# A planned attention kernel: prologue shared by two engines and two queues, projections mixed in and bunched, last norm and last residual divided

## The chip, the cores and the metric

The kernel runs on one core of one Trainium2 chip. The metric is the device time of one execution in microseconds (us); medians are of three to nine executions. Besides the time, each execution has a span (first to last instruction of the core) and a mean granted clock of TensorE. Differences below one microsecond in the times are not read as anything here.

Engine names in the profile: PE is TensorE, PEld its weight loads, DVE VectorE, ACT ScalarE, POOL GpSimd, SP SyncE.

## The reference

```python
x  = A_x                                   # [1, 2048, 512] bf16
xn = layernorm(x)                          # over the 512 columns, eps 1e-5
q  = (xn @ wq) as 32 heads of 16           # wq 512 x 512
k, v = xn @ wk, xn @ wv                    # one k and one v for all heads, 512 x 16
p  = softmax(q k^T / 4)                    # 32 heads, 2048 x 2048
s  = (p v, heads side by side) @ wo        # wo 512 x 512
h  = silu(xn @ w1)                         # w1 512 x 1792
g  = silu(h @ w2)                          # w2 1792 x 512
return x + s * g
```

## The kernel before

The kernel does not write its instructions in program order. It holds tasks with estimated durations, a clock for each engine, and rules that choose what comes next; from the resulting order it writes the instructions of each engine and the semaphores between them. So a constant in a rule moves thousands of instructions. What is planned is this work:

- Scores: 32 heads by 4 blocks of 512 queries by 16 tiles of 128 keys, in all 2048 "slots" of 128 keys by 512 queries. One score phase of TensorE makes three or four slots at once, each in a quarter of the array's rows.
- Exponentials: a real Exp on ScalarE into one of `NPA` buffers, or a fast path (VectorE writes the bits of a bf16 exponential, GpSimd adds three shifted copies, so that one slot then needs four PV matmuls instead of one).
- PV: "rounds" of four matmuls that fill four column strips of one bank.
- Projections q, h (first of the feed-forward), z (second) and w (output): "jobs" made of rounds of the same four-column kind.

```python
MM = 216.0                                  # ns of a round or a score phase
NEAR, AHEAD = 12, 0.6
NPA, PRESS = 22, 16                         # buffers of P; number in use at which PV goes first
NDB, NDS = 6, 8                             # buffers of fast-path bits, of shifted copies
START_Z, START_H = 8, 14                    # a job starts only below this number of P buffers in use
WIDE, NMIN, EARLY = 2, 3, 200.0             # banks that one Exp may take
...
def s_mm(pe, b, g, i, kt):                  # one slot's scores
    return pe.matmul(bank(b), lhsT=kt_sb[32 * i:32 * i + 32, g % 2, kt * P:(kt + 1) * P],
                     rhs=qt_sb[32 * i:32 * i + 32, (g // 2) % NQR, :],
                     start=True, stop=True, tile_position=(32 * i, 0))

def col4(h, b, lhs, rhs, start, stop, n=NQ):    # one round
    for j in range(4):
        last = h.matmul(bank(b)[32 * j:32 * (j + 1), 0:n], lhsT=lhs(j), rhs=rhs, start=start, stop=stop,
                        tile_position=(0, 32 * j), skip_group_check=True)
    return last
```

The prologue loads x, normalises 16 token tiles in four groups (statistics, reciprocal root, xn; then TensorE transposes it and projects k, v and the first q). Keys come free group by group, and with them slots:

```python
for t in range(4):
    dma(SP, "x", x_tile(t), xv[:, t, :], 128, [xkey(t)], prio=0)
...
for t in range(4):
    mk_T([t], t)          # transposes of xn, token tile t
mk_K(0, 0, 1, 4)          # k of tile 0
mk_q(0)                   # q of the first 512 queries, after all four tiles
mk_K(0, 1, 4, 3)          # k of tiles 1 to 3
mk_V(0)
for c in range(1, NC):    # the other three groups of keys
    mk_T([4 * c, 4 * c + 1]); mk_T([4 * c + 2, 4 * c + 3])
    mk_K(c, 4 * c, 4 * c + 4)
    mk_V(c)
NPRO = len(jobs)          # jobs start in the order of the list: projections only after all of these
```

TensorE's rule, at every step: a score phase if one can go and ScalarE will need it; otherwise one round, chosen so:

```python
if pr and pr[0] == "go" and (a_pressure() >= PRESS or closing()):
    col = ("pv", pr[1])
elif jr[0] == "go":
    col = ("job", jr[1])
elif pr and pr[0] == "go":
    col = ("pv", pr[1])
elif tr and tr[0] == "go":
    col = ("tail", None)
elif t_done and not tail["made"]:
    ...                   # filler: matmuls on zeros, meant to keep TensorE busy
```

The tail: after the last PV the last 512 queries are normalised (transpose, reciprocal, product, transpose on VectorE), the output projection of four token tiles follows, then VectorE scales and adds the residual, and four stores end it:

```python
tail["items"].sort(key=lambda x: (x[0], x[1], x[2]))   # 12 rounds with o < 3 first, then four with o = 3
...
t1 = Task(DV, T_P, lambda v: v.scalar_tensor_tensor(out=fin_sb[:, k, :], in0=bank(b), scalar=0.25,
          in1=tmp_sb[:, tt % 8, :], op0=ALU.mult, op1=ALU.mult), ...)
t2 = Task(DV, 333.0, lambda v: v.tensor_tensor(ob_sb[:, tt % 4, :], fin_sb[:, k, :], xr_sb[:, tt % 4, :], ALU.add), ...)
```

The softmax here doesn't subtract the row's maximum and nothing guards it: scores larger than these inputs give would overflow.

## Time and profile before

| | before |
|---|---|
| median of 3 | 684.39 us (684.32 to 685.62) |
| span of the profiled execution | 684.2 us, clock 0.996 |
| busy TensorE, ScalarE, VectorE, GpSimd | 98, 96, 88, 80% |
| first Exp | 13.31 us |
| first score phase after 48 slots, "slot 48" below (all keys nearly in use) | 38.57 us |
| slot 2020 issued (28 left, this one included) | 661.52 us |
| last PV begins, span ends | 674.83, 684.2 us |

The prediction below shows the page's totals, stretches and waits of this kernel. Two views more are used later. First the chain that ended last, by engine: the work, followed back from the end, lies on TensorE for 54% of the span and on ScalarE for 35%, so by this view neither is the sole owner.

```profile
PE 54%; ACT 35%; DVE 9%; issue 1%; DMA 1%; SPq 0%; DVEq 0%
```

The time line: start, length, engine, line, operation, output from inputs, shapes, count, and in brackets the idle time before with what ended it.

### The profile page before, as it was taken

What the parts mean: (1) busy time and instruction counts of PE and PEld (TensorE: products, weight loads), DVE (VectorE), ACT (ScalarE), POOL (GpSimd) and SP (SyncE); (2) the same over time, 40 slices, a digit from 0 to 9 for tenths busy, and PEclk for the clock granted to TensorE, in tenths of its full rate; (3) what the DMA queues carried; (4) which work ended last, traced back from release to release, by engine and by line L of the source; (5) the groups of instructions that cost most, each with busy time, mean ns of one, the idle gap of its engine ahead of it and who ended that gap; (6) DMA issues with size and microseconds to landing.
All of it is one profiled execution on the core that took longest, in us unless ns stands there. A gap on an engine that the chain in (4) does not pass through costs nothing.

```text
span 684.2 us, 21033 instructions
## 1 busy us (share of the span) xinstructions
PE 668.1 (98%) x8887; PEld 191.7 (28%) x8887; DVE 603.0 (88%) x1064; ACT 658.8 (96%) x763; POOL 548.8 (80%) x545
## 2 busy tenths in 40 slices
PE   8899999999999999999999999999999999999995
PEld 3422222222222222222222222222222222222221
DVE  9889999898899998988989899899889999898863
ACT  4899999999999999999999999999999999999994
POOL 2059989789998878889878788889999778899980
PEclk9999999999999999999999999999999999999999
DMA  9300000000000010000000100000000010000000
GB/s 307 128 17 2 3 2 2 2 2 2 2 2 17 18 33 1 2 2 2 2 2 1 34 17 17 2 2 1 2 2 2 2 33 16 17 3 2 2 2 32
DMA packets 11436, 12.65 MB, mean 18 GB/s; under 512 B 1808, under 2 KB 10768, under 8 KB 11344
## 3 DMA queue, kind: packets, MB, share of 16 engines
q1 hardware_dynamic: 10288, 11.28, 5.1%
q8 instruction: 72, 1.18, 0.7%
q10 hardware_dynamic: 1056, 0.03, 0.1%
q14 instruction: 20, 0.16, 0.1%
HBM read 8.95 MB, written 2.10 MB: 16 GB/s over the span
## 4 chain that ended last, share of the span: by engine, by line
PE 54%; ACT 35%; DVE 9%; issue 1%; DMA 1%; SPq 0%; DVEq 0%
ACT pa_sb L1365 33%; PE ps L1103 22%; PE ps L789 19%; PE ps L479 14%; DVE db_sb L975 4%; ACT t_sb L601 2%; DVE stats_sb L426 1%; DVE f_sb L1120 1%; DVE u_sb L603 1%; DMA ds_sb<-in_A_x_dram 1%; DVE xn_sb L455 0%; DVE otr_sb L1124 0%; DVE xnT_sb L506 0%; DVE tmp_sb L603 0%; SPq L373 0%
## 5 line engine op out<-in xcount | busy, mean ns | idle before, releaser
L1042 POOL INT64_ADD ds_sb<-db_sb x534 | 544.9, 1040 | 117.8 <-DVE db_sb L975 65.2
L1365 ACT ACTIVATE pa_sb<-ps 128x1024 bf16<-128x1024 f32 (+1 forms) x684 | 630.5, 1027 | 6.8 <-PE ps L789 6.3
L975 DVE TENSOR_SCALAR db_sb<-ps 128x512 uint16<-128x512 f32 x712 | 468.6, 684 | 61.4 <-PE ps L789 57.7
L1103 PE MATMUL ps<-ds_sb,v_sb 128*32 128x512 bf16 x2136 | 277.5, 383 | 0.0
L789 PE MATMUL ps<-qt_sb,kt_sb 32*128 32x512 bf16 x2048 | 258.0, 385 | 4.9 <-ACT pa_sb L1365 1.7
L1103 PE MATMUL ps<-pa_sb,v_sb 128*32 128x512 bf16 x1336 | 244.6, 384 | 1.4 <-ACT pa_sb L1365 1.4
L1103 PE MATMUL ps<-db_sb,v_sb 128*32 128x512 bf16 x712 | 186.5, 384 | 1.1 <-DVE f_sb L1120 1.1
L789 PEld LDWEIGHTS ps<-qt_sb,kt_sb 32*128 32x128 bf16 x2048 | 64.2, 91 | 283.3 <-ACT pa_sb L1365 181.8
L1103 PEld LDWEIGHTS ps<-ds_sb,v_sb 128*32 128x32 bf16 x2136 | 69.1, 95 | 54.0 <-issue 35.3
L479 PE MATMUL ps<-xnT_sb,w_sb 128*32 128x512 bf16 x896 | 75.4, 385 | 0.0
L479 PE MATMUL ps<-w_sb,u_sb 128*32 128x512 bf16 x896 | 73.1, 384 | 0.0
L1103 PEld LDWEIGHTS ps<-pa_sb,v_sb 128*32 128x32 bf16 x1336 | 60.5, 95 | 44.5 <-issue 29.9
L1103 PEld LDWEIGHTS ps<-db_sb,v_sb 128*32 128x32 bf16 x712 | 46.3, 95 | 22.3 <-issue 14.5
L601 ACT ACTIVATE t_sb<-ps 128x512 bf16<-128x512 f32 x72 | 45.3, 629 | 0.0
L603 DVE SCALAR_TENSOR_TENSOR u_sb<-t_sb,ps 128x512 bf16<-128x512 bf16 x56 | 38.1, 681 | 1.5 <-ACT t_sb L601 0.2
L1120 DVE STREAM_TRANSPOSE f_sb<-ps 128x512 f32<-128x512 f32 x32 | 22.6, 707 | 9.3 <-PE ps L1103 9.2
L479 PEld LDWEIGHTS ps<-xnT_sb,w_sb 128*32 128x32 bf16 x896 | 17.9, 94 | 26.9 <-issue 22.0
L479 PEld LDWEIGHTS ps<-w_sb,u_sb 128*32 128x32 bf16 x896 | 16.9, 94 | 26.3 <-issue 24.5
L479 PE MATMUL ps<-xnT_sb,wq_sb 128*32 128x512 bf16 x256 | 21.0, 392 | 0.0
L479 PE MATMUL ps<-wo_sb,on_sb 128*32 128x512 bf16 x256 | 20.8, 383 | 0.1
L1124 DVE TENSOR_TENSOR otr_sb<-f_sb,rcp_sb 128x256 bf16<-128x256 f32 x32 | 13.3, 417 | 0.3
L603 DVE SCALAR_TENSOR_TENSOR tmp_sb<-t_sb,ps 128x512 bf16<-128x512 bf16 x16 | 10.8, 677 | 2.0 <-ACT t_sb L601 1.9
(52 smaller groups left out, 140.4 us busy)
## 6 DMA issues: line engine op xcount, KB each, us to landing
w_sb<-in_B_w_dram SPq DMA_DIRECT2D x2, 1792.0 KB, 12.8
xr_sb<-in_A_x_dram SPq DMA_DIRECT2D x16, 128.0 KB, 2.3
out_dram<-ob_sb SPq DMA_DIRECT2D x16, 128.0 KB, 1.7
ds_sb<-in_A_x_dram SPq DMA_DIRECT2D x3, 512.0 KB, 7.1
ds_sb<-in_A_x_dram SPq DMA_DIRECT2D x4, 128.0 KB, 2.5
wq_sb<-in_A_wq_dram SPq DMA_DIRECT2D x1, 512.0 KB, 4.9
wo_sb<-in_A_wo_dram SPq DMA_DIRECT2D x1, 512.0 KB, 14.6
kt_sb<-kt_sb SPq DMA_DIRECT2D x4, 64.0 KB, 2.3
```

Source lines behind the costliest of these rows:

```text
L426: ts_ = pl.add(Task(DV, 593.0, lambda v, t=t: v.bn_stats(stats_sb[:, t, :], x_tile(t)), [xkey(t)], [("st", t)], 1 + j, gate=(lambda: q_don ...
L479: last = h.matmul(bank(b)[32 * j:32 * (j + 1), 0:n], lhsT=lhs(j), rhs=rhs, start=start, stop=stop, tile_position=(0, 32 * j), skip_group_c ...
L601: t1 = Task(AC, 490.0, lambda a: a.activation(t_sb[:, k, :], src, ACT.Tanh, scale=scale), [held], [("t", k)], 0, [t0])
L603: t2 = Task(DV, T_P, lambda v: v.scalar_tensor_tensor(out=dst, in0=t_sb[:, k, :], scalar=1.0, in1=src, op0=ALU.add, op1=ALU.mult), [held, ...
L789: return pe.matmul(bank(b), lhsT=kt_sb[32 * i:32 * i + 32, g % 2, kt * P:(kt + 1) * P], rhs=qt_sb[32 * i:32 * i + 32, (g // 2) % NQR, :], ...
L975: bt.P[i] = pl.add(Task(DV, T_P, lambda v, b=b, i=i, bb=bt.b: v.tensor_scalar(db_sb[:, bb, i * NQ:(i + 1) * NQ], bank(b), 128.0 * LOG2E, 1 ...
L1042: whole["po"].append(pl.add(Task(PO, T_P64, lambda g, cols=cols: g.int64_add(ds_sb[:, s, cols].bitcast(U64), db_sb[:, bt.b, cols].bitcast( ...
L1103: h = pe.matmul(bank(OB)[32 * i:32 * (i + 1), :], lhsT=lhs, rhs=rhs, start=s0, stop=s1, tile_position=(0, 32 * i), skip_group_check=True)
L1120: t1 = pl.add(Task(DV, T_TR, lambda v: v.transpose(f_sb[:, k, :], bank(OB)), [("ps", OB)], [("F", k)], 1, [norm.get(("m", g - 2))]))
L1124: t3 = pl.add(Task(DV, 332.0, lambda v: v.tensor_tensor(o3[:, :, val:val + DH], f3[:, :, val:val + DH], rcp_sb[:, k, :].unsqueeze(2).to_br ...
L1365: op = pl.place(AC, 0.8333 * NQ * n + T_AF, lambda a: a.activation(pa_sb[:, s * NQ:(s + n) * NQ].rearrange("p (b n) -> p b n", n=NQ), ps3[ ...
```

## The change

Its intent: start the first Exp and each later group of keys sooner by taking work off VectorE in the prologue and putting feed-forward rounds into TensorE's idle time there; plan the middle with more P buffers and with projections in bunches (fewer changes of layout); shorten the tail by splitting the last norm and by letting TensorE and ScalarE add the residual of three tiles. A random factor with a fixed seed on some thresholds picks one plan of many. Left out of the cut below are another bank for the PV sums (7 for 6) and new time estimates of the planner (450 ns for issuing a DMA, where it had 60). The diff, cut to its core:

```diff
+J_BASE, J_END, MIXJ = 0.1, 1.0, 2
+SEED, SPREAD = 17, 0.1
-NEAR, AHEAD = 12, 0.6
+NEAR, AHEAD = 18, 0.6
-NPA, PRESS = 22, 16
-NDB, NDS = 6, 8
+NPA, PRESS = 26, 16
+PRESS_Z, PRESS_H = 18, 16
+NDB, NDS = 5, 8
-START_Z, START_H = 8, 14
-WIDE, NMIN, EARLY = 2, 3, 200.0
+START_Z, START_H = 6, 8
+WIDE, NMIN, EARLY = 3, 3, 200.0
 ...
-            dma(SP, "x", x_tile(t), xv[:, t, :], 128, [xkey(t)], prio=0)
+            dma((SP, AC)[t % 2], "x", x_tile(t), xv[:, t, :], 128, [xkey(t)], prio=-2)
 ...  # statistics of tile 1 on ScalarE: sum by Copy, sum of squares by Square
+        m1 = pl.add(Task(AC, 700.0, lambda a: a.activation(f_sb[:, 0, :], x_tile(1), ACT.Copy, scale=1.0 / D,
+                                                          accum_out=mv_sb[:, 1, 0:1]), ...
 ...  # q of the first queries per token tile, copied by ScalarE; two xnT copies on ScalarE, not three
-        for t in range(4):
-            mk_T([t], t)
+        mk_T([0], 0)
+        mk_T([1], 1)
         mk_K(0, 0, 1, 4)
-        mk_q(0)
-        mk_K(0, 1, 4, 3)
+        mk_q0(0, 3, 5)
+        mk_T([2], 2)
+        mk_T([3], 3)
+        mk_q0(3, 4, 6)
+        mk_K(0, 1, 4)
 ...  # projections may start while prologue jobs are still to come
-            while st["job"] < len(jobs):
+            while st["pro"] < NPRO or st["job"] < len(jobs):
+                if st["pro"] < NPRO and can_start(jobs[st["pro"]], True):
+                    jb = jobs[st["pro"]]
+                    st["pro"] += 1
+                elif st["job"] < len(jobs) and (st["pro"] >= NPRO or xn_task[4 * MIXJ - 1].op is not None) and can_start(jobs[st["job"]], False):
 ...  # PV goes ahead of a job at 18 buffers in use for z, 16 for the rest
+            lim = vary(PRESS if jr[0] != "go" else PRESS_Z if jr[1].kind == "z" else PRESS_H)
-            if pr and pr[0] == "go" and (a_pressure() >= PRESS or closing()):
+            if pr and pr[0] == "go" and (a_pressure() >= lim or closing()):
 ...  # tail
+            if g == NG - 1:
+                return last_norm(g, oi, k, f3, o3, den, val)      # the same four steps, each in two halves
+                src = fin_sb[:, tt % 2, :] if part else xr_sb[:, tt % 4, :]
+                pl.place(PE, MM, lambda pe: pe.matmul(bank(4 + r), lhsT=ident[:, :], rhs=src, start=part == 0, stop=part == 1), ...
+                    t2 = pl.add(Task(AC, 490.0, lambda a: a.activation(ob_sb[:, tt % 4, :], bank(4 + r), ACT.Copy), ...
```

## The prediction

> **What bounds the kernel now.** The work is 2048 slots. A slot is one score tile of 128 keys by 512 queries: a score matmul (L789), an exponential, and PV matmuls that add into one bank (L1103). The exponential of a slot goes one of two ways. On ScalarE it is a real Exp (L1365), followed by one PV matmul. On the fast path VectorE writes the bits of a bf16 exponential (L975), GpSimd adds three shifted copies (L1042), and four PV matmuls follow. I read the page first, for the engines' totals and the costliest groups:
>
> ```profile
> PE 668.1 (98%) x8887; PEld 191.7 (28%) x8887; DVE 603.0 (88%) x1064; ACT 658.8 (96%) x763; POOL 548.8 (80%) x545
> L1365 ACT ACTIVATE pa_sb<-ps 128x1024 bf16<-128x1024 f32 (+1 forms) x684 | 630.5, 1027 | 6.8 <-PE ps L789 6.3
> ```
>
> TensorE and ScalarE both look full, so shares do not decide which one bounds. Next, busy time by stretches, which shows that the two ends are another matter than the middle (columns: stretch, length, busy of PE, PEld, DVE, ACT, POOL, clock, DMA share, GB/s):
>
> ```profile
> 8.80:32.00 23.20, 20.46 (x358) 11.58 (x358) 21.83 (x75) 17.86 (x28) 0.00 (x0) 1.00 0.67 232
> 300.00:400.00 100.00, 99.88 (x1338) 27.78 (x1330) 89.28 (x147) 99.87 (x115) 85.65 (x85) 1.00 0.03 10
> 660.00:684.20 24.20, 17.20 (x239) 5.58 (x234) 9.85 (x20) 14.77 (x21) 6.14 (x6) 0.95 0.07 23
> ```
>
> The prologue is VectorE's (21.83 of 23.20 us; layer norm of 16 tiles), the middle is shared by TensorE and ScalarE. The time line of the middle gives TensorE's price of a phase, that of the start the moments at which scores begin, and ScalarE's rows its idle time:
>
> ```profile
> 310.10 0.39 PE L789 MATMUL ps<-qt_sb,kt_sb 32*128 32x512 bf16 x3
> 310.42 0.61 PE L479 MATMUL ps<-w_sb,u_sb 128*32 128x512 bf16 x8
> 310.97 0.39 PE L789 MATMUL ps<-qt_sb,kt_sb 32*128 32x512 bf16 x3
> ...
> 12.87 0.73 PE L789 MATMUL ps<-qt_sb,kt_sb 32*128 32x512 bf16 x6
> 23.26 0.39 PE L789 MATMUL ps<-qt_sb,kt_sb 32*128 32x512 bf16 x3 [0.76 <-DVE kt_sb L535]
> 38.57 0.61 PE L789 MATMUL ps<-qt_sb,kt_sb 32*128 32x512 bf16 x3
> 661.52 0.39 PE L789 MATMUL ps<-qt_sb,kt_sb 32*128 32x512 bf16 x3
> ...
> 13.31 7.14 ACT L1365 ACTIVATE pa_sb<-ps 128x1024 bf16<-128x1024 f32 x10 [0.16 <-PE ps L789]
> 23.70 9.06 ACT L1365 ACTIVATE pa_sb<-ps 128x1024 bf16<-128x1024 f32 x13 [3.25 <-PE ps L789]
> ```
>
> From 310.10 to 310.97, one cycle of a score phase and two rounds of four column matmuls takes 0.87 us; cycles with three rounds take 1.09. So a round is about 0.2165 us, a score phase of three or four slots the same, and each change between the two layouts costs 0.11 us. The first exponential is at 13.31; ScalarE then runs dry for 3.25 us because the second group of keys is late (23.26).
>
> The waits between 40 and 660 us and the chain that ended last complete it:
>
> ```profile
> PEld ps L789 <- ACT pa_sb L1365: 174.8, 413, 0.4
> PEld ps L789 <- DVE db_sb L975: 78.7, 176, 0.6
> ACT pa_sb L1365 <- PE ps L789: 2.0, 7, 0.5
> ...
> 654.73 10.13 ACT pa_sb L1365 x11
> 675.25 0.73 DVE f_sb L1120
> 676.75 0.72 DVE on_sb L1131
> 677.52 1.08 PE ps L479 x16
> 681.05 0.42 DVE ob_sb L656
> 681.46 0.33 DVEq L312
> ```
>
> The wait of 174.8 us is mostly no wait: 413 times 0.42, which is the usual space between the weight loads before and after a change of layout. ScalarE's 2.0 us says that it is hardly ever starved. Its price is 10.13/11 = 0.921 us for two slots; one tile of 512 takes about 0.49 to 0.54.
>
> **What the Trainium skill says.** "TensorEngine Tiling (Array Packing)", Key Properties: changing the tiling mode drains TensorE. The trace agrees, with 0.11 us per change, and the count of changes is therefore a cost of its own. "ScalarE: Activation LUTs", What ACT_TABLE_LOAD costs: an ACTIVATE takes 186 ns + 0.833 ns per element, 93 ns more per pointer operand, and neighbours overlap by 93 ns. For 1024 elements that is 1039 ns and a pitch of 946; the trace has 1046 and 921. So a wider instruction saves some 0.07 to 0.09 us, no more. "DMA: Bandwidth & Descriptors", Issuing engines are not separate DMA queues: a second issuing engine saves only issue time. Issues on SyncE here take about 0.43 us each, and the fourth tile of x is first used at 5.72.
>
> **The change part by part.** I counted instructions by kind in the two compiled programs. Durations are those above.
>
> 1. *Start.* Tiles 1 and 3 of x go out from ScalarE's queue, so the fourth leaves two issues (0.9 us) earlier. ScalarE takes tile 1's statistics (two passes of 512 and a small one, some 1.7 us by the page's formula, ending near 5.4). The instruction order on VectorE still puts three statistics ahead of the rstd steps, so these start at about 5.7 instead of 6.33: 0.6 us. Two instead of three xnT copies on ScalarE, and q per token tile (four 128-column rounds and a 128-column copy after the last tile, instead of 1.04 us of matmuls and 0.67 us of VectorE), save another 1.6. First Exp at about 11.0 instead of 13.3.
> 2. *Second keys.* Before, eight statistics of later tiles (0.66 each) ran on VectorE ahead of tiles 4 to 7's copies; now two do. With the start 0.2 us earlier that puts the second keys at 23.3 - 4 = about 19.3. The 16 slots that the first keys allow take ScalarE, four times three wide, some 7.2 us, to 18.2; the gap of 3.25 shrinks to about 1.5, and perhaps 0.5 comes at the third keys. Slot 48 was issued at 38.57; with singles at 0.52 us I put it near 36.2. Gain 2.4. Three rounds of h and one of q more are done by then, in TensorE time that was idle or filler.
> 3. *Middle, slots 48 to 2020.* Fast-path slots rise from 712 to 732, real Exp slots fall from 1336 to 1316. ScalarE: 20 x 0.46 = -9.2 us. TensorE pays three more PV matmuls for each, 60/4 = 15 rounds or 3.2 us, over the whole run. Counted for these slots: before 632 score phases, 1564.5 column rounds, 1264 changes; after 621, 1553.8, 1242. That is 2196.5 x 0.2165 + 1264 x 0.11 = 614.6 us, against 2174.8 x 0.2165 + 1242 x 0.11 + 0.4 = 607.8: -6.8 us. (More phases of four slots, 110 against 76, are why phases fall; some rounds have only moved out of this stretch.) The stretch took 661.52 - 38.57 = 623.0 us, so TensorE had 8.4 us of slack. ScalarE's own sum there is about 615 before and 605 after. Both limits fall together, TensorE's less. I keep most of the slack: about 615.5 after, gain 7.5.
> 4. *End, slot 2020 to the last PV.* ScalarE paces it in both (28 slots and up, 13.7 us before). But 15 rounds of the second projection and 6 more PV rounds now lie here: TensorE's sum before the last PV goes from some 10.6 to about 14.1 us. Loss 1.0.
> 5. *Tail.* The transpose, reciprocal, product and transpose took 0.73 + 0.27 + 0.44 + 0.72 plus issue, 2.23 us to 677.48. In halves the first half of on_sb is there some 0.35 us earlier. Three of four residual sums (0.42 each) leave VectorE for a TensorE matmul and a ScalarE copy; VectorE then has four scalings of 0.6 and one sum, 2.9 us instead of 3.5 after the first matmuls. Gain 1.1. The last store stays.
>
> Sum: 2.4 + 7.5 - 1.0 + 1.1 = 10.0. Selection of such a plan by search should have cut slack as well, so I add 0.8: 684.4 - 10.8 = 673.6 us.
>
> **The rivals.** (a) TensorE alone bounds: the 20 moved slots only turn ScalarE's time into PV rounds, the slack stays at 8.4 or grows. For it: 20 slots cost 3.2 us of TensorE, and its sum falls by 1 us only over the whole program. Then only start, tail and moved work count: 677 to 679 us. (b) VectorE or GpSimd becomes the bound. GpSimd runs 549 shifts instead of 534, 571 us of some 625; the buffers of fast-path bits go from 6 to 5, and VectorE instructions that wait for GpSimd before writing one rise from 76 to 95. Against it: VectorE waited 57.7 us for scores, GpSimd 65.2 us for bits. If it happens, score phases stall: 678 to 684 us. (c) The slack goes, since more P buffers (26 for 22) and bunched projections free the order: 610 us in the middle, 667 to 670 us in all. (d) The weights of h stall the prologue, since TensorE now needs them near 20 us. They were issued at 4.7 and the two big loads took 11.9 and 13.8 us to land, so by 18.5 at the latest; I expect no stall.
>
> **Range and chances.** The middle carries the spread: its slack can be 4 to 13 us, and start and tail add about 1.5 either way. So 669 to 679 holds it 8 times in 10. The line of 2% is 670.7; only rival (c) gets there, 0.2. Nothing above loses 2% without a stall that no view shows: 0.01.
>
> **What would show it.** First Exp near 11.0 and second keys' scores near 19.3 (steps 1 and 2). Slot 48 near 36.2; middle near 615, with about 621 changes' pairs at an unchanged 0.87 us cycle (step 3). ScalarE's waits for scores growing past 2.0 us speak for (a); VectorE's or TensorE's waits for GpSimd, for (b). Last ScalarE Exp to end of span under 10.4 us (steps 4 and 5). The prediction is wrong if the cycle itself gets longer, or if the middle moves by less than 4 or more than 12 us.

## More of the kernel before

From the last PV's start, 674.83, it takes 3.14 us to the first scaling, and the last residual sum is done at 681.80.

```profile
674.83 0.39 PE L1103 MATMUL ps<-pa_sb,v_sb 128*32 128x512 bf16 x1
674.83 3.74 PE L479 MATMUL ps<-wo_sb,on_sb 128*32 128x512 bf16 x56
...
677.97 1.29 DVE L653 SCALAR_TENSOR_TENSOR fin_sb<-ps,tmp_sb 128x512 bf16<-128x512 f32 x2 [0.51 <-PE ps L479]
...
681.05 0.75 DVE L656 TENSOR_TENSOR ob_sb<-fin_sb,xr_sb 128x512 bf16<-128x512 bf16 x2
```

## The result, and the profile after

The changed kernel took 678.47 us (median of 4, 677.87 to 679.16); before, beside it, 684.59 (median of 4, 684.32 to 685.62). A ratio here is the mean time of one kernel's fast runs over the mean of the other's fast runs of the same rounds, so it is not quite the ratio of the medians: 0.9908, with a 95% interval of 0.9891 to 0.9925. That is a gain of 0.9%, inside the range of the prediction, but only 6.1 us where 10.8 were expected. The profiled spans are 684.2 and 677.3 us, at clocks of 0.996 and 0.997.

The page after (busy time and instructions by engine; the group of Exps; the chain by engine):

```profile
PE 663.9 (98%) x8941; PEld 192.1 (28%) x8941; DVE 610.0 (90%) x1081; ACT 655.1 (97%) x763; POOL 564.9 (83%) x561
...
PE 76%; ACT 12%; DVE 9%; issue 1%; DMA 0%; ACTq 0%
...
L1518 ACT ACTIVATE pa_sb<-ps 128x1024 bf16<-128x1024 f32 (+2 forms) x674 | 621.4, 1019 | 8.9 <-PE ps L847 7.9
```

The shares of busy time hardly differ. The chain does: TensorE now owns 76% of it and ScalarE 12, where they had 54 and 35. ScalarE's idle time ahead of Exps, 6.8 us before, is 8.9. The stretches of the prologue and the middle (columns as in the prediction):

```profile
8.80:32.00 23.20, 19.91 (x386) 10.04 (x383) 22.16 (x74) 19.40 (x29) 0.00 (x0) 1.00 0.67 235
300.00:400.00 100.00, 99.71 (x1335) 27.39 (x1336) 92.53 (x154) 99.29 (x113) 90.33 (x90) 1.00 0.02 5
```

VectorE still fills the prologue, 22.16 of 23.20 us. The moments at which keys come free, first ScalarE's rows of the time line:

```profile
12.00 5.48 ACT L1518 ACTIVATE pa_sb<-ps 128x1536 bf16<-128x1536 f32 x4
...
20.93 3.03 ACT L1518 ACTIVATE pa_sb<-ps 128x1024 bf16<-128x1024 f32 x4 [1.44 <-PE ps L847]
...
29.95 8.35 ACT L1518 ACTIVATE pa_sb<-ps 128x512 bf16<-128x512 f32 x13 [1.05 <-PE ps L847]
```

Then TensorE's score phases:

```profile
20.49 0.39 PE L847 MATMUL ps<-qt_sb,kt_sb 32*128 32x512 bf16 x3 [0.58 <-DVE kt_sb L559]
...
29.51 0.39 PE L847 MATMUL ps<-qt_sb,kt_sb 32*128 32x512 bf16 x3 [0.55 <-DVE kt_sb L559]
...
36.83 0.39 PE L847 MATMUL ps<-qt_sb,kt_sb 32*128 32x512 bf16 x4 [0.51 <-DVE kt_sb L559]
38.03 0.39 PE L847 MATMUL ps<-qt_sb,kt_sb 32*128 32x512 bf16 x3 [0.51 <-DVE db_sb L1039]
```

The first Exp is at 12.00, 1.3 us earlier than before; the second keys' scores at 20.49, 2.8 us earlier. But the third and fourth groups of keys wait for VectorE's copy of k as well, and slot 48 goes out at 38.03, only 0.54 us earlier than in the profile of before (whose half clock falls just there, see below). The waits between 40 and 655 us (total, times, longest):

```profile
PEld ps L847 <- ACT pa_sb L1518: 149.4, 352, 0.4
PEld ps L847 <- DVE db_sb L1039: 101.7, 228, 0.7
...
ACT pa_sb L1518 <- PE ps L847: 4.7, 16, 0.6
```

The first two rows together are 580 weight loads at 0.43 us, the usual space around a change of layout; before, between 40 and 660 us, they were 589. ScalarE's wait for scores has grown from 2.0 to 4.7 us, which is small but is the sign that the prediction named for its rival (a). The tail, rows of TensorE, VectorE and ScalarE:

```profile
668.08 0.39 PE L1177 MATMUL ps<-pa_sb,v_sb 128*32 128x512 bf16 x1
668.23 3.48 PE L503 MATMUL ps<-wo_sb,on_sb 128*32 128x512 bf16 x60
...
669.82 0.76 DVE L1207 STREAM_TRANSPOSE on_sb<-otr_sb 128x256 bf16<-128x256 bf16 x2
671.10 2.61 DVE L702 SCALAR_TENSOR_TENSOR fin_sb<-ps,tmp_sb 128x512 bf16<-128x512 f32 x4 [0.52 <-PE ps L503]
...
673.60 1.19 ACT L1386 ACTIVATE ob_sb<-ps 128x512 bf16<-128x512 f32 x2 [0.28 <-PE ps L1381]
```

The last PV starts at 668.08. The norm in halves ends at 670.58, yet the first scaling starts only at 671.10, when TensorE's rounds of the output projection release it: 3.02 us after the last PV, against 3.14 before. The last ScalarE copy ends at 674.79, 3.69 us after the first scaling; before, the last VectorE sum ended 3.83 us after it.

**Where TensorE's time went.** To see it by stage I counted, in the compiled order of each kernel, the score phases, rounds and changes of layout, and gave them the prices that the time line shows (0.2165 us for a phase or a round, 0.11 for a change, and in the prologue about 0.06 for a transpose and 0.03 for a matmul of v). Filler on zeros is not counted. The rest of each stage is idle time of TensorE. These sums carry an error of about 2 us, which is why one stage comes out slightly negative.

| kernel | span | counted work | idle to slot 48 | slots 48 to 2020 | to the last PV | to the end |
|---|---|---|---|---|---|---|
| before | 684.2 | 647.7 | 19.1 | 8.4 | 2.8 | 6.3 |
| after | 677.3 | 647.7 | 16.8 | 9.2 | -1.0 | 4.6 |

A recount from the two traces, four matmuls to a round, gives 18.1, 8.5, 3.5 and 6.3 us of idle time before and 16.1, 8.9, -0.1 and 4.5 after, with 647.8 and 647.9 us of work: the same picture without the negative stage.

TensorE does the same amount of work in both, within the error: 12 score phases (2.6 us) and 17 changes (1.9) less, 15 rounds (3.2) and the tail's six residual matmuls (1.3) more. So the whole gain of 6.9 us in the span of the profiled executions is idle time taken from TensorE: 2.3 at the start, 3.8 while the last Exps run and 1.7 in the tail, with the middle unchanged within the error. The middle did get shorter (622.9 to 616.9 us), because its count fell from 614.6 to 607.7: phases and changes were saved there and rounds moved out, and the counts of the three other stages rose by 1.7, 3.7 and about 1.6.

Some of this idle time is clock. The stretch at half speed runs from 36.5 to 39.9 us in the profile of before and from 39.6 to 43.0 in that of the changed kernel (columns as above; the third number from the end is the clock). First before, then after:

```profile
36.50:39.50 3.00, 3.00 (x26) 0.49 (x22) 2.12 (x4) 2.24 (x4) 2.34 (x3) 0.50 0.20 34
```

```profile
39.60:42.90 3.30, 3.30 (x30) 0.65 (x26) 1.85 (x3) 3.06 (x6) 2.64 (x3) 0.50 0.15 26
```

In before 2.1 us of it lie ahead of slot 48, with TensorE busy without a gap. At full speed slot 48 would have gone out some 1 us sooner there (an estimate: half of the 2.1), so this profile does not show that the changed kernel reaches slot 48 any earlier, and the start's share of the gain is nearer 1.3 than 2.3 us. In the changed kernel the stretch lies in the middle and costs about 1.2 us: the run with the tail undone below, which has the same order and no such stretch, needs 615.6 us for the middle and not 616.9. Without the stretch the spans are 682.4 (most executions of before) and 676.1 us, a gain of 6.3.

### The profile page after: what moved, and what is told of

It is laid out like the page before. It is cut to its first block, busy times and chain, and to the rows that moved or that the text cites. A ratio compares the mean times of both kernels' runs of the same rounds, so it can differ in the third digit from the quotient of the medians.

```text
span 677.3 us, 21172 instructions
## 1 busy us (share of the span) xinstructions
PE 663.9 (98%) x8941; PEld 192.1 (28%) x8941; DVE 610.0 (90%) x1081; ACT 655.1 (97%) x763; POOL 564.9 (83%) x561
## 4 chain that ended last, share of the span: by engine, by line
PE 76%; ACT 12%; DVE 9%; issue 1%; DMA 0%; ACTq 0%
PE ps L1177 32%; PE ps L847 26%; PE ps L503 18%; ACT pa_sb L1518 11%; DVE db_sb L1039 3%; DVE stats_sb L450 1%; DVE u_sb L652 1%; ACT t_sb L650 1%; DVE xn_sb L479 0%; DVE xnT_sb L530 0%; DVE f_sb L1224 0%; DMA ds_sb<-in_A_x_dram 0%; DVE fin_sb L702 0%; DVE otr_sb L1228 0%; DVE kt_sb L559 0%
## 5 line engine op out<-in xcount | busy, mean ns | idle before, releaser
L1106 POOL INT64_ADD ds_sb<-db_sb x549 | 559.2, 1040 | 98.5 <-DVE db_sb L1039 43.1
L1518 ACT ACTIVATE pa_sb<-ps 128x1024 bf16<-128x1024 f32 (+2 forms) x674 | 621.4, 1019 | 8.9 <-PE ps L847 7.9
L1039 DVE TENSOR_SCALAR db_sb<-ps 128x512 uint16<-128x512 f32 x732 | 474.9, 683 | 47.3 <-PE ps L847 40.6
L847 PE MATMUL ps<-qt_sb,kt_sb 32*128 32x512 bf16 x2048 | 253.5, 385 | 5.9 <-ACT pa_sb L1518 1.8
L1177 PE MATMUL ps<-db_sb,v_sb 128*32 128x512 bf16 x732 | 178.4, 384 | 0.6 <-DVE f_sb L1224 0.6
L503 PE MATMUL ps<-xnT_sb,w_sb 128*32 128x512 bf16 x896 | 72.9, 386 | 0.0
L503 PE MATMUL ps<-w_sb,u_sb 128*32 128x512 bf16 x896 | 70.7, 384 | 0.0
L1177 PEld LDWEIGHTS ps<-db_sb,v_sb 128*32 128x32 bf16 x732 | 43.8, 95 | 18.3 <-issue 12.5
L503 PE MATMUL ps<-xnT_sb,wq_sb 128*32 128x512 bf16 x240 | 19.5, 384 | 0.0
```

Source lines behind the costliest of these rows:

```text
L1039: bt.P[i] = pl.add(Task(DV, T_P, lambda v, b=b, i=i, bb=bt.b: v.tensor_scalar(db_sb[:, bb, i * NQ:(i + 1) * NQ], bank(b), 128.0 * LOG2E, 1 ...
L1106: whole["po"].append(pl.add(Task(PO, T_P64, lambda g, cols=cols: g.int64_add(ds_sb[:, s, cols].bitcast(U64), db_sb[:, bt.b, cols].bitcast( ...
L1177: h = pe.matmul(bank(OB)[32 * i:32 * (i + 1), :], lhsT=lhs, rhs=rhs, start=s0, stop=s1, tile_position=(0, 32 * i), skip_group_check=True)
L1518: op = pl.place(AC, 0.8333 * NQ * n + T_AF, lambda a: a.activation(pa_sb[:, s * NQ:(s + n) * NQ].rearrange("p (b n) -> p b n", n=NQ), ps3[ ...
```

## The experiments

After this reading the questions were which part of the change gives the gain, whether TensorE's time alone has a price now, and whether better plans exist. Twelve kernels ran, all correct; before took 684.29 to 684.65 us (medians) beside them. The kernels that undo a part start from the changed one. The expectations name the theories in their own words; in short, one holds that the middle's constants carry the gain and TensorE is what bounds, its rivals that the start or the tail carries it, that ScalarE bounds as much, or that a plan found by search is luck. Every run but those of the tail and the four that lengthen an engine also gets a new plan of the whole program, so each stands for its part by one plan alone.

**The middle undone.** Constants of the middle and the seed as before; prologue, mixing and tail kept.

```diff
-J_BASE, J_END, MIXJ = 0.1, 1.0, 2
-SEED, SPREAD = 17, 0.1
+J_BASE, J_END, MIXJ = 0.6, 1.0, 2
+SEED, SPREAD = 0, 0.1
-NEAR, AHEAD = 18, 0.6
+NEAR, AHEAD = 12, 0.6
-NPA, PRESS = 26, 16
-PRESS_Z, PRESS_H = 18, 16
+NPA, PRESS = 22, 16
+PRESS_Z, PRESS_H = 16, 16
-NDB, NDS = 5, 8
+NDB, NDS = 6, 8
-START_Z, START_H = 6, 8
+START_Z, START_H = 8, 14
-WIDE, NMIN, EARLY = 3, 3, 200.0
+WIDE, NMIN, EARLY = 2, 3, 200.0
```

> Only the planner's constants of the middle go back (start and tail of the change are kept). Theory 1, the gain is made in the middle by fewer score phases and layout changes: about 684 us (683 to 686), that is nearly the whole gain of 6 us gone. Theory 2, the gain is made by the shared prologue and the projections mixed into it: 679 to 681 us.

Measured: 685.31 us (684.93 to 686.10), ratio to before 1.0016 (0.9999 to 1.0033). The whole gain is gone. By the count, TensorE's idle time at the start and end is as low as in the changed kernel or nearly so (17.0, 0.4 and 4.4 us), but in the middle it is 12.6 where it was 8.4 before, and the counted work is 0.8 higher. So a better start and end with the old constants only hand their time to the middle. In this plan the constants are not a part that adds its own share; without them the other parts are worth nothing.

**The start undone.** Prologue as before and no mixing; middle and tail kept.

```diff
-            dma((SP, AC)[t % 2], "x", x_tile(t), xv[:, t, :], 128, [xkey(t)], prio=-2)
+            dma(SP, "x", x_tile(t), xv[:, t, :], 128, [xkey(t)], prio=0)
 ...  # wke copy, memset of kt, statistics of tile 1, gate of statistics, xnT copies, order of jobs: as before
-                elif st["job"] < len(jobs) and (st["pro"] >= NPRO or xn_task[4 * MIXJ - 1].op is not None) and can_start(jobs[st["job"]], False):
+                elif st["job"] < len(jobs) and (st["pro"] >= NPRO or False) and can_start(jobs[st["job"]], False):
```

> Only the prologue goes back (one DMA queue, all statistics on VectorE, q as one job, projections not mixed into it); constants and tail are kept. Theory 1: 679 to 681 us, since slot 48 is issued only half a microsecond earlier with the new prologue. Theory 2: 683 to 685 us. Counted from its program the middle loses 4.4 us of TensorE time too, so a time of 682 to 683 would leave both open.

Measured: 681.99 us (681.81 to 682.21), ratio 0.9964 (0.9949 to 0.9979), 3.5 us over the changed kernel's median. That lies between what the two theories expected and decides for neither. Its idle time is 18.0, 8.3, 1.6 and 4.5 us in the four stages: start and last Exps each lose part of what the change had gained there.

**The tail undone.** Last norm whole, all residual sums on VectorE.

```diff
-            if g == NG - 1:
-                return last_norm(g, oi, k, f3, o3, den, val)
 ...
-            tail["sums"] = [(r, part) for part in range(2) for r in range(3)]
 ...  # reads of the last rounds: the whole on_sb, not halves
-                if r < 3:
+                if r < 0:
                     stt[r] = pl.add(scaled(tt, r))
                 else:
                     for tk in final(tt, r):
```

> Only the tail goes back (last norm whole, residual on VectorE); the order of everything before it is the same. Theory that the tail is bounded by TensorE's 12 rounds of the output projection and then by four scalings in a row: 678.4 to 679 us, tail from last PV to end within 0.4 us of the change's 9.2. Theory of the prediction (halves and TensorE sums worth 1.1 us): 679.5 us and a tail of 10.3.

Measured: 678.26 us (678.00 to 678.37), ratio 0.9909 (0.9894 to 0.9924): the same as the changed kernel. The order of the middle is the same in both, so this is a clean comparison, as the expectation of a tail bounded by TensorE's rounds had it. Its tail:

```profile
666.98 3.59 PE L503 MATMUL ps<-wo_sb,on_sb 128*32 128x512 bf16 x60
...
669.98 1.29 DVE L702 SCALAR_TENSOR_TENSOR fin_sb<-ps,tmp_sb 128x512 bf16<-128x512 f32 x2 [0.51 <-PE ps L503]
```

From the last PV (666.84) to the first scaling it takes 3.14 us, 0.12 more than with the divided norm, and 9.4 us to the end, against 9.2. All of the division of the tail is worth 0.2 us in the trace and nothing in the times.

**The bunching undone.** Only the thresholds at which jobs start and at which z yields to PV.

```diff
-PRESS_Z, PRESS_H = 18, 16
+PRESS_Z, PRESS_H = 16, 16
-START_Z, START_H = 6, 8
+START_Z, START_H = 8, 14
```

> Only the three thresholds that bunch the projections go back (when a projection may start, when PV goes first). Theory 1: 681 to 683 us, with 653 score phases instead of 646. Theory 2: within 1 us of 678.5.

Measured: 682.79 us (682.18 to 683.27), ratio 0.9975 (0.9960 to 0.9990): 4.3 us of the gain go with these three numbers. The plan has 653 score phases (646 with bunching, 658 before), the counted work is 648.2, and the idle time of the middle is 10.6 us instead of 9.2. Bunching saves a little work and a little idle time; both are visible. The changed kernel's 9.2 hold some 1.2 us of half clock, which this profile does not have; set against 8.0 (the run with the tail undone) the middle accounts for 2.6 of the 4.3, the work for 0.5, and the stage of the last Exps for 1.0. How much of this is the draw of the plan was not tried.

**The price of TensorE's and ScalarE's time.** Four kernels add a known amount to one engine, spread over the program, two on the kernel before and two on the changed one. On TensorE every sixteenth score phase is issued twice (the same matmuls into the same bank, the result unchanged). On ScalarE every sixth Exp is preceded by a small Exp of 12 columns into an otherwise unused tile.

```diff
-            def emit(pe, mm=tuple(mm)):
+            st["sph"] = st.get("sph", 0) + 1
+            def emit(pe, mm=tuple(mm) * (2 if st["sph"] % 16 == 0 else 1)):
```

```diff
+                def emit(a, more=st["xph"] // 6 if st["xph"] % 6 == 0 else 0, s=s, n=n, b0=b0, b1=b1, step=step):
+                    if more:
+                        a.activation(dead_sb[:, more * 12 - 12:more * 12], ps3[:, b0, 0:12], ACT.Exp)
```

TensorE on the kernel before, 41 phases:

> The kernel before with the score matmuls of every 16th score phase issued twice (same banks, same values): 41 x 0.2165 = 8.9 us more TensorE time, nothing else moved. If TensorE bounds the middle, about +8 us (692 to 693); if ScalarE bounds it and TensorE has real slack, +0 to +3.

ScalarE on the kernel before, 114 small Exps:

> The kernel before with a small extra Exp (12 columns into a dead tile) ahead of every 6th exponential: 114 x some 0.08 to 0.10 us = 9 to 11 us more ScalarE time. If ScalarE bounds the middle, +8 us or more; if TensorE does, +0 to +4. If both are full by turns, +5 to +8 here and in the TensorE run.

TensorE on the changed kernel, 40 phases:

> The changed kernel with every 16th score phase issued twice: 40 x 0.2165 = 8.7 us. If the change has moved the bound to TensorE (the chain gives it 76% where it had 54%): +8 to +9 (686 to 687.5), the full price. If ScalarE still bounds: under +4.

ScalarE on the changed kernel, 112 small Exps:

> The changed kernel with the extra small Exp ahead of every 6th exponential: 112 x 0.08 to 0.10 = 9 to 11 us of ScalarE time. If the bound has moved to TensorE: +0 to +4 us and clearly less than in the kernel before; if ScalarE's relief made the gain, +8 or more as before.

The amount on TensorE is phases times 0.2165 us. That on ScalarE is read from the trace, since it was less than I had expected: the next Exp starts 0.060 to 0.078 us after the small one, 0.060 in the median, and summed over the trace the 114 add 7.4 us and the 112 as much. A doubled phase, from its start to the next round, takes 0.537 us and a single one 0.321, which confirms the 0.2165. In ScalarE's rows of the lengthened kernel before:

```profile
310.34 0.34 ACT L1370 ACTIVATE dead_sb<-ps 128x12 bf16<-128x12 f32 x1
310.40 2.11 ACT L1371 ACTIVATE pa_sb<-ps 128x1024 bf16<-128x1024 f32 x2
```

| added to | amount | median | ratio to before | what it cost | share paid |
|---|---|---|---|---|---|
| TensorE, before | 8.9 us | 693.98 | 1.0131 (1.0111 to 1.0150) | 9.0 us | 100% |
| ScalarE, before | 7.4 us | 690.00 | 1.0070 (1.0053 to 1.0087) | 4.8 us | 65% |
| TensorE, after | 8.7 us | 685.93 | 1.0017 (1.0000 to 1.0034) | 7.5 us | 86% |
| ScalarE, after | 7.4 us | 681.14 | 0.9940 (0.9921 to 0.9959) | 2.2 us | 30% |

The cost is the difference of ratios (to 1 for the kernel before, to 0.9908 for the changed one) times 684.9 us, the mean time of before in that call; the intervals make each share uncertain by some 15 points in the two rows of before and by 20 to 25 in those of after, which rest on two intervals. Executions of like clock set side by side (0.997, and 1.000) give 8.0 and 8.1 us for TensorE on the changed kernel and 2.6 to 2.8 for ScalarE, so about nine tenths and a little over a third. TensorE's time had about its full price in both kernels. ScalarE's had about two thirds of its price before and about a third after. The chain by engine says the same, here of the kernel before with more ScalarE work and of the changed kernel with the same addition:

```profile
ACT 76%; PE 17%; DVE 5%; DMA 1%; issue 1%; SPq 0%; DVEq 0%
```

```profile
PE 54%; ACT 37%; DVE 6%; issue 1%; POOL 1%; DMA 0%; ACTq 0%
```

So the change has moved the kernel away from ScalarE's limit and left it at TensorE's. These are prices of time added; what time taken away from one engine alone would give, no run tried.

**Mixing undone.** Only this: projections wait until all prologue jobs have started.

```diff
-                elif st["job"] < len(jobs) and (st["pro"] >= NPRO or xn_task[4 * MIXJ - 1].op is not None) and can_start(jobs[st["job"]], False):
+                elif st["job"] < len(jobs) and (st["pro"] >= NPRO or False) and can_start(jobs[st["job"]], False):
```

> The changed kernel, only the mixing goes back: a projection may start only when all jobs of the prologue have started. Counted over the program TensorE's work is the same as in the change (646 to 647 score phases, 1653 rounds). If TensorE's total issue time sets the time, 678.4 us as the change; if it is the idle time at the start that the mixed-in projections fill (6 rounds of 0.2165 us less before slot 48, so more later), 680 to 682 us. The theory that the new prologue's speed alone matters says 678.4.

Measured: 680.74 us (680.67 to 680.96, 5 runs), ratio 0.9936 (0.9922 to 0.9950), 2.3 us over the changed kernel. This run explains the start. Slot 48 goes out at 36.4 us here, 2.2 earlier than in the profile of before (some 1 us of which is its half clock), while in the changed kernel mixing takes 1.6 of that back. VectorE's rows show how, first without and then with mixing, and TensorE's row of slot 48 without it:

```profile
23.77 0.69 DVE L450 BATCH_NORM_STATS2 stats_sb<-ds_sb 128x6 f32<-128x512 bf16 x1
24.37 1.27 DVE L530 COPY xnT_sb<-ps 128x1024 bf16<-128x1024 bf16 x2
...
27.48 0.68 DVE L559 CAST kt_sb<-ps 128x512 bf16<-128x512 f32 x1
...
36.41 0.39 PE L847 MATMUL ps<-qt_sb,kt_sb 32*128 32x512 bf16 x3 [0.18 <-DVE db_sb L1039]
```

```profile
23.78 1.28 DVE L450 BATCH_NORM_STATS2 stats_sb<-ds_sb 128x6 f32<-128x512 bf16 x2
24.98 0.67 DVE L652 SCALAR_TENSOR_TENSOR u_sb<-t_sb,ps 128x512 bf16<-128x512 bf16 x1
25.57 0.68 DVE L530 COPY xnT_sb<-ps 128x1024 bf16<-128x1024 bf16 x1
...
28.77 0.68 DVE L559 CAST kt_sb<-ps 128x512 bf16<-128x512 f32 x1
```

The rounds of h lie in TensorE's idle time, but each finished h needs a step on VectorE (0.67 us), and VectorE sets the pace of the prologue. The third keys' copy slips from 27.48 to 28.77, the fourth from 34.24 to 36.08. About half of the first slip is the step of h; the other half is a second statistics (0.6 us) that this plan puts ahead of the copies of xnT. Yet mixing is a gain in all: without it the work that was not done at the start is paid at the end. The time from the last PV to the end of the span is 12.4 us instead of 9.2, with 14 rounds of the second projection after the last PV that the changed kernel had done by then.

**The tail in another order.** The changed kernel's tail waits for TensorE's twelve first rounds. Here the last round of a token tile is issued as soon as its half of the norm is there, and the scalings get four buffers instead of two (dead xn buffers serve).

```diff
-            for n, (_, r, o, emit) in enumerate(tail["items"][:1]):
+            first = {}                       # the next round of each token tile
+            for n, it in enumerate(tail["items"]):
+                if it[1] not in first:
+                    first[it[1]] = n
+            for n in sorted(first.values(), key=lambda n: (-tail["items"][n][0], n)):
+                _, r, o, emit = tail["items"][n]
 ...
+        def fin_of(tt):
+            if tt >= NT - 2:
+                return xn_sb[:, tt % 4, :], ("xn", tt % 4)
+            return fin_sb[:, tt % 2, :], ("fin", tt % 2)
```

> The changed kernel, only its last 9 us differ: the last output-projection rounds of tiles 0 and 1 go before the remaining rounds of the others as soon as the first half of the last norm is there, and the four scalings get four buffers instead of two. If the tail is bounded by TensorE's 12 rounds and then by the scalings, last PV to end falls from 9.2 to about 8.7 us and the time by 0.5 us (677.9); if by the store alone, nothing.

Measured: 678.88 us (678.23 to 679.78), ratio 0.9909 (0.9892 to 0.9925): no gain, where 0.5 us were expected. The work did end earlier, in ScalarE's row:

```profile
672.85 1.58 ACT L1396 ACTIVATE ob_sb<-ps 128x512 bf16<-128x512 f32 x3 [4.69 <-PE ps L1391]
```

The last PV starts at 668.21, so the last copy is done 6.2 us after it, against 6.7 in the changed kernel. But the last two stores took 2.8 and 2.7 us from issue to landing, where no store of the changed kernel's tail took over 2.0. That the stores now go out closer together (0.4 to 0.5 us apart) is not the cause: in the two runs that follow, with the same tail and the same spacing, all four landed in 1.7 to 1.9 us, and their tails still take 9.1 us from the last PV to the end, as before the reordering (9.2).

**Two plans from a search.** Since the constants and the random factor pick one plan of many, some 3000 plans were built and ranked by the planner's own clock, with the tail in the other order. The shortest was run, and the second-best of an independent search:

```diff
# first
-J_BASE, J_END, MIXJ = 0.1, 1.0, 2
-SEED, SPREAD = 17, 0.1
+J_BASE, J_END, MIXJ = 0.1, 1.2, 2
+SEED, SPREAD = 69481, 0.1
-NEAR, AHEAD = 18, 0.6
+NEAR, AHEAD = 20, 0.6
-WIDE, NMIN, EARLY = 3, 3, 200.0
+WIDE, NMIN, EARLY = 3, 3, 300.0
# second
+J_BASE, J_END, MIXJ = 0.1, 0.6, 3
+SEED, SPREAD = 58946, 0.3
+HOLD, Q_LEAD = 1000.0, 3.0          # was 3.3
+PRESS_Z, PRESS_H = 18, 17
+WIDE, NMIN, EARLY = 3, 3, 300.0
```

> Tail as in the run before, and constants and random seed of the planner found by a search over some 3000 plans, the shortest by the planner's own clock (1.8 us shorter than with the tail alone). Theory that TensorE's idle time is what is left to gain and that the planner sees it: 676 to 677 us. Theory that plans picked by their own clock are mostly luck: within 0.5 us of the run before.

> As the run before with the second-best plan of an independent search (other seed, larger random spread, 644 score phases, mixing from the third group of tiles). Same two theories: 676 to 677 us, or within 0.5 us of the tail alone. If the two plans differ by more than 1 us, the planner's clock does not rank them.

Measured: 676.24 us (675.47 to 676.66), ratio 0.9868 (0.9853 to 0.9884), and 675.97 us (675.96 to 675.99), ratio 0.9866 (0.9851 to 0.9880). Both beat both kernels, and they lie 2.6 and 2.9 us under the run with the same tail, where the theory that such picks are luck had expected 0.5 at most. The second is 1.3% under before and 2.5 us under the changed kernel; all its runs had a clock of 1.000, and against the changed kernel's two runs at 1.000 the gain is 1.9 us. In it mixing starts one group of keys later (`MIXJ` 3): the third keys' copy is back at 27.47 us and slot 48 at 37.1.

Beside the two kernels, the counted work and idle time of the rest (columns as above):

| kernel | span | counted work | idle to slot 48 | slots 48 to 2020 | to the last PV | to the end |
|---|---|---|---|---|---|---|
| middle undone | 683.0 | 648.5 | 17.0 | 12.6 | 0.4 | 4.4 |
| start undone | 679.9 | 647.5 | 18.0 | 8.3 | 1.6 | 4.5 |
| tail undone | 676.2 | 646.3 | 16.8 | 8.0 | -1.0 | 6.1 |
| bunching undone | 680.4 | 648.2 | 16.8 | 10.6 | 0.0 | 4.8 |
| mixing undone | 678.9 | 648.1 | 17.1 | 11.2 | -2.2 | 4.8 |
| second plan from the search | 674.2 | 646.8 | 16.9 | 8.0 | -2.0 | 4.5 |

The span is the sum of the five, up to rounding. None of the six profiled executions has the half-clock stretch. The work stays within 2.2 us in all of them; what differs is idle time of TensorE, by 9 us between the best and the kernel before. In the middle it ranges from 8.0 to 12.6, and why one plan has more of it than another was not taken apart. Since other draws and small shifts of constants moved the time by almost 3 us in the searched plans, a part of the 2.3 to 4.3 us that single parts cost above may be the draw of the plan; no part was undone with a second seed.

## Why the prediction was right or wrong

The time fell into the range, and "within 2%" was right. The centre was 4.9 us too low. In the spans of the profiled executions, 10.8 us of gain were predicted and 6.9 came (6.3 without the half clock). The measured 678.5 lies near the upper end of the range, where the prediction put its rival (a): the range held by its width and not by what stands behind its centre. The steps, with the gain in us:

| step | predicted | measured | miss |
|---|---|---|---|
| 1 and 2, start to slot 48 | 2.4 | 0.5 | -1.9 |
| 3, middle | 7.5 | 6.1 | -1.4 |
| 4, slot 2020 to the last PV | -1.0 | 0.1 | +1.1 |
| 5, tail | 1.1 | 0.2 | -0.9 |
| "I add 0.8" for the search | 0.8 | 0 | -0.8 |
| sum | 10.8 | 6.9 | -3.9 |

The 0.5 at the start includes some 1 us by which half clock delays the profile of before, so the first miss is if anything larger.

- **Step 1, "First Exp at about 11.0".** It came at 12.00, so 1.3 of 2.3 us. Of the 0.6 us for an earlier reciprocal root 0.2 came: the step that writes the first guess (rstd_sb) ran at 6.35 instead of 6.55, and the first xn at 7.74 instead of 7.93. VectorE's second statistics waited for a tile of x until 4.25, and ScalarE's of tile 1 lasted to 5.31, so neither the second queue nor the second engine brought the group forward by much. Of the 1.6 us from transposes and q per token tile 1.1 came. (The terms of the prediction's own formula for ScalarE's three instructions, 613, 706 and 187 ns, add to 1.5 us and not 1.7; they took 1.8, with two more that read the accumulator.)
- **Step 2, the term that failed most.** Second keys "at about 19.3" came at 20.49. The prediction took eight later statistics off VectorE ahead of these keys; the trace of before has seven, and in the changed kernel the eight small steps from var_sb to rstd_sb, from 12.88 to 14.71 us, start some 0.2 us apart with little between, where before they had run among statistics, so leaving these out did not free their whole time. Then "three rounds of h and one of q more are done by then, in TensorE time that was idle or filler" was true of TensorE and wrong as a cost: their evacuation went to VectorE, which the prediction itself had called the prologue's engine. The run without mixing reaches slot 48 at 36.4, almost the predicted 36.2; with mixing it is 38.0. So the prediction's 36.2 is what the prologue gives when the work that it counted as free is not there.
- **Step 3, the size.** The count was right: -6.8 predicted, 614.6 to 607.7 or -6.9 in the end. Idle time in the middle was said to fall a little ("I keep most of the slack", 615.5) and came out between 8.0 and 9.2 us where it had been 8.4. The half-clock stretch costs the changed kernel's middle about 1.2 us and that of before, which has 1.3 us of it, about 0.7 (half of that stretch, an estimate). So some 0.5 of the 1.4 us is the clock.
- **Step 3, the reason.** "Both limits fall together, TensorE's less" was the wrong emphasis. In the changed kernel only about a third of added ScalarE time is paid, and nearly all of TensorE's, so ScalarE's limit fell past the point where it counts; that the last of its 9.2 us bought little is argued from this, not shown by a run. TensorE's work over the whole program did not fall at all (647.7 and 647.7). By the count the gain is work moved from a full stage into stages in which TensorE had idled. Rival (a) said this, "only start, tail and moved work count: 677 to 679 us", and the time fell where it put it; but its premise, TensorE alone, does not hold for the kernel before, where two thirds of added ScalarE time were paid. One price was also misread: 10.13/11 = 0.921 us of an Exp takes in the full length of the last one; from start to start the trace of before has 0.905 in the median.
- **Step 4, "Loss 1.0", wrong in sign.** TensorE had 2.8 us of idle time while ScalarE paced the last Exps (3.5 by the recount). The 3.7 us of work that were moved in filled it, and the stage took 13.2 us instead of 13.3. The prediction had the TensorE sum right (10.6 to 14.1 foreseen, 10.5 to 14.2 counted) and ScalarE's pace of 13.7 us beside it, and added a loss that the two do not give.
- **Step 5, "Gain 1.1".** Both halves of the argument lacked a limit. The divided norm is done 0.13 us earlier after the last PV than the whole one (2.50 against 2.63), but twelve of TensorE's rounds, 2.60 us, lie between the last PV and the first scaling (eleven with o below 3 and the first with o = 3) and release it. And the residual sums moved to TensorE and ScalarE end up in series behind the scalings: matmul, copy and their waits take what the VectorE sums had taken. The run with the tail undone shows that nothing is lost without it.
- **"Selection ... I add 0.8".** There was no sign of it. Search does find such plans, as the last two runs show, but this plan had not got it.
- **The other rivals.** (b) did not happen: VectorE's waits for GpSimd before writing fast-path bits were 2.2 us in total between 40 and 655 us. (c), the slack gone, is refuted by 9.2 us of idle time (8.0 without the half clock). (d), late weights of h, did not show: the first of the two big loads had landed at 17.3 and the rounds of h began at 21.3. (Its "by 18.5" puts the longer landing time on the earlier issue; the second load goes out at 10.0 and lands at 24.0.)

What stays open: the idle time of 8 to 12 us in the middle, which differs between plans; how the 3.5 us of the start divide between the quicker prologue and mixing beyond the 2.3 of mixing alone, since the parts do not add; how much of each part's worth is the draw of one plan; why the half-clock stretch comes in some executions and not in others, which no run here shows; and why two stores of one run landed late.

## What to carry to other kernels

Where two engines look full, lengthen each by a known amount: here one paid all of it and the other about two thirds, which no share of busy time told. Count the bounding engine's work by stage before and after; when the count is the same and the clock too, the gain can only be idle time filled, and a stage in which the engine waits for another (the prologue, the last exponentials) is where work is best put. Work put into one engine's idle time still needs its followers on other engines, so charge it to the engine that paces that stage, and re-tune the rules of the middle together with the ends, since each alone can be worth nothing.

## What the Trainium skill lacked or had wrong

- "TensorEngine Tiling (Array Packing)", Key Properties, says that a change of tiling mode drains TensorE but gives no time for it. Here it is about 0.11 us per change, some 1300 changes or 143 us of a program of 680.
- "ScalarE: Activation LUTs" says that an ACTIVATE can give an accumulator output but not what this costs. Here each is a second instruction of 0.19 us, after 0.63 us for a Copy of 512 columns and 0.72 for a Square whose bias is a pointer.
- The same page's formula gives a pitch of about 103 ns for a small Exp of 12 columns (186 + 10 - 93). Between full-size Exps the next one started 60 to 80 ns after it. For 1024 columns the formula's 946 ns compare with 905 (median in the kernel before).
- No page has it: with TensorE 98% and ScalarE 96% busy, time added to TensorE was paid in full and time added to ScalarE to 65%; after the change, to 86% and 30%.
- No page has what one late stretch at half clock costs such a kernel: here it lasted 3.41 us, came between 36 and 43 us in the two kernels' profiles and not at all in others, and the changed kernel took 679.1 us at a mean clock of 0.997 against 677.9 at 1.000.
